# A fused attention, gating and MLP kernel: plain float32 scores and zero products in the first batch, earlier loads, and a clamp moved to GpSimd

## The chip, the cores and the metric

The kernel runs on one core of one Trainium2 chip. The metric is the device time of one launch in microseconds (us). The kernel before takes 788.62 us, the median of three runs (787.88 to 788.93). Engines are named as the profile names them: PE is TensorE (matrix products), PEld its weight loads, DVE is VectorE, ACT is ScalarE, POOL is GpSimd, SP is the engine whose queue issues all DMAs here.

## The reference

Three stages, in float32, for 4 batches of 576 positions:

```python
# 1: causal attention with a decay, 8 heads of 64 (32 heads in all)
scores = q @ k.T / 8 ; bias = -(cum[i] - cum[j]), cum = cumsum(max(s, 0))
scores = where(causal, -1e9, scores + min(bias, 0))
attn = exp(scores - max) / (sum + 1e-9) ; x = attn @ v      # heads side by side: 576 x 512
# 2: gated product
gate = sigmoid(causal 5-tap convolution of x, per channel) ; x = (gate * (x @ w_val)) @ w_out
# 3: mixing along the sequence at rank 32, then a two-layer MLP
u = x + (x.T @ U @ V).T ; out = u + max(u @ w_ch1, 0) @ w_ch2        # 512 -> 2048 -> 512
```

The inputs of stages 2 and 3 come as 64-bit floats, so weights are read as pairs of 32-bit words.

## The kernel before

**Precision.** PE can take a float32 operand whole, or in a reduced form (`F32R`). Most products here run in the reduced form on a high and a low part of each operand: the rounded value and the rest. For scores this means two products: row block Q1 with K1 (high parts, and four rows that carry the decay) and Q2 with K2 (the cross terms). A head listed in `WHOLE` (line 85) skips this: q and k go straight into Q1 and K1, and one plain float32 product makes a score block. In the trace a plain product stands as two MATMUL records.

**Splitting q and k.** For a head not in `WHOLE`, `load_head` (line 274) loads q and k into one tile `qk` by two DMAs, and `prep_head` (line 296) makes `hi` on ACT (`qk_hi`), the rest on POOL (`qk_lo`, tile Q2), and issues five DMAs on SP's queue that put the parts where the products want them. `load_head(n + 1)` stands at the start of step n of the main loop (line 736), so `qk` is loaded one head ahead.

**A head.** Five query chunks. `score` makes a chunk's scores, DVE masks them and takes the row minimum (`nm`; tile P), ACT takes the exponential (with the sum), `trans` transposes P in up to four blocks of 128 by 128 through a PSUM tile `pt`, six groups to a head, ACT or DVE copies them out to PTA or PTB, and `attn_v` multiplies with V for two heads at once (`av`). `norm_rows` (line 546) brings the sums of a pair of heads into rows: DVE makes a reciprocal, POOL spreads it (`wrs`), PE transposes it, and ACT or DVE copies it back. `norm` (line 564) then makes X, its high and low part (`xh` on POOL, `xl` on POOL), and the gate by five taps.

**Side work.** Weights are widened from 64-bit words by `widen` (line 350), nine steps for each half: scale on ACT (`wd_a`), clamp on DVE (`wd_lim`), four bit operations on DVE (`wd`), rounding, rest and low part on POOL. In the attention stage this goes step by step beside the heads. From 330 us on, `widen_w` (line 807) does the rest of the MLP weights, two halves for each of 14 blocks; each half starts with a DMA of 512 KB into the tile `raw`.

**Dense work.** From the ninth head on, stages 2 and 3 (up to `u`) of the batch before run beside the heads; the MLP itself (`ch1`, `ch2`: tiles `d`, `hh`, `hl`, `acc`) begins around 330 us and fills the rest.

**What sets the order.** `PLAN` and `FIRST` give the engine and a priority to each kind of work; `defer` holds work back by the planner's own clock with the delays in `DT`. A scheduler then orders each engine's instructions. Each engine, and SP's queue of DMA issues, runs its list in order; an instruction that waits holds up all behind it.

Of the kernel before, what the change touches and what calls it, by code (L numbers as in the profile page):

```python
# [11 lines left out]
F32 = mybir.dt.float32  # L12
# [21 lines left out]
    "ul": ("gpsimd", -6000),  # L34
    "u4": ("vector", 0),
    "wd_a": ("scalar", 6000),
    "wd_lim": ("vector", -100),
    "wd": ("vector", -2000),
    "wd_hi": ("gpsimd", -2000),
    "wd_lo": ("gpsimd", 2000),  # L40
# [41 lines left out]
RING = 7  # L82
PACED = False
SIDE = [7, 7, 3, 7]
WHOLE = [0, 1, 2, 3, 16, 30]
PB = [1, 1, 1, 2, 2]
XB = 1
FIRST = {"pt41": ["scalar", 500], "nl": ["vector", 500], "xh": ["gpsimd", 2000], "c2": ["tensor", 100], "max": ["vector", 2000], "rs": ["vector", 500], "t": ["tensor", 100], "rb": ["vector", 500], "av": ["tensor", 6000], "wd_rest": ["gpsimd", 2000]}
ORDER0 = "T0 S0 T1 T4 S1 T3 T2 S2 S3 S4"
ORDER = "T0 T1 S0 T2 T3 S1 S2 S3 T4 S4 A0 A1"  # L90
NPD = 6
DT = {"exp": 0.51, "xh": 0.96, "xl": 0.25, "tap": 1.5, "taps": 0.9, "tanh": 1.83, "gv": 4.3, "nl": 3.6, "rows": 7.68, "prep": 1.51}
WARM = 13


# [1 line left out]
def fused_kernel(ctx, tc, qT, kT, vP, s, wval, wout, convw, U, V, w1, w2, rows01, out):  # L97
# [173 lines left out]

    hd = {}

    def load_head(n, direct=False):
        b, h = divmod(n, H)
        t = hd[n] = {"K": 64 + KP if n else 66, "nm": at.tile([P, 6], F32, tag="nm", name="nm")}
        kind = F32 if n in WHOLE else F32R
        for nm in ("Q1", "K1"):
            t[nm] = at.tile([64 + KP, S], kind, tag=nm, name=nm)
        if n in WHOLE:  # L280
            q, k = t["Q1"][0:64, :], t["K1"][0:64, :]
        else:
            t["qk"] = at.tile([P, S], F32, tag="qk", name="qk")
            q, k = t["qk"][0:64, :], t["qk"][64:, :]
        nc.sync.dma_start(q, qT[b, h])
        nc.sync.dma_start(k, kT[b, h])
        if n:
            for i, nm in enumerate(("Q1", "K1")):
                nc.sync.dma_start(t[nm][64:, :].bitcast(F32), EF[i][n:n + 1] if direct else ef[n, i])
# [87 lines left out]
    def pairs(t):  # L377
        return t.bitcast(U32).rearrange("p (n two) -> p n two", two=2)
# [78 lines left out]
        side_work.append(lambda j=j: widen_half(j))  # L457


    def score(n, c):  # L460
        t = hd[n]
        W, q0, r = CW[c], Q0[c], QN[c]
        regions = [(0, W)] if c < 4 else [(0, HS), (HS, S)]
        shift = S - P - (W - r if c else 0)
        nm = t["nm"]
        pr = Pt[c][n % PB[c]]
        force("sc", 1)
        worst = 3.0e38
        for i, (k0, k1) in enumerate(regions):
            ps = psD.tile([P, 512], F32, tag="d", name="sc")  # L470
            o = ps[:, 0:k1 - k0]
            if n in WHOLE:
                K = t["K"]
                Via("s").matmul(o, t["Q1"][0:K, q0:q0 + P], t["K1"][0:K, k0:k1], start=True, stop=True)
            else:
                Via("s").matmul(o, t["Q1"][:, q0:q0 + P], t["K1"][:, k0:k1], start=True, stop=False)
                Via("s").matmul(o, t["Q2"][:, q0:q0 + P], t["K2"][:, k0:k1], start=False, stop=True)
            last = k1 == W
            least = nm[0:r, c:c + 1] if last else nm[0:r, 5:6]

            Via("max").tensor_tensor_reduce(
                pr[0:r, k0:k1], o[0:r, :], causal[0:r, k0 + shift:k1 + shift], -0.125, worst,
                op0=ALU.add, op1=ALU.min, accum_out=least,
            )
            worst = least

        def exp():
            Via("exp").activation(
                pr[0:r, 0:W], pr[0:r, 0:W], AF.Exp, bias=nm[0:r, c:c + 1], scale=-1.0,
                accum_out=sums[n // 2 % 2][0:r, c, n % 2:n % 2 + 1],  # L490
            )
            ready.add(("P", n, c))
        defer(DT["exp"] + W / 960.0, exp, "sc")

    def trans(n, c):
        w, q0 = QN[c], Q0[c]
        nblk = c + 1
        until(("P", n, c))
        if c == 0:
            hd[n]["PTA"] = at.tile([P, 4 * DA], F32, tag="PTA", name="PTA")  # L500
            hd[n]["PTB"] = at.tile([P, 5, S - SA], F32, tag="PTB", name="PTB")
        groups = [(0, nblk)] if nblk <= 4 else [(0, 3), (3, 5)]
        for b0, b1 in groups:
            force("pt", 1)
            ps = psD.tile([P, 512], F32, tag="d", name="pt")
            for j in range(b0, b1):
                Via("t").transpose(ps[:, (j - b0) * P:(j - b0 + 1) * P], Pt[c][n % PB[c]][:, j * P:(j + 1) * P], ident)
            if q0 < SA:
                dst = hd[n]["PTA"][:, q0:q0 + b1 * DA].rearrange("p (j w) -> p j w", w=DA)[:, b0:b1, 0:w]
            else:  # L510
                dst = hd[n]["PTB"][:, b0:b1, q0 - SA:q0 - SA + w]
            src = ps[:, 0:(b1 - b0) * P].rearrange("p (j w) -> p j w", w=P)[:, :, 0:w]
            rnd(f"pt{c}{b0 // 3}", dst, src)
# [32 lines left out]
    def norm_rows(pr):  # L546
        force("sc")
        sm = sums[pr % 2]
        rs = at1.tile([P, 5, 2], F32, tag="rs", name="rs", bufs=2)
        Via("rs").tensor_scalar_add(rs, sm, 1e-9)  # L550
        Via("rs").reciprocal(rs, rs)
        wide_rs = at1.tile([P, 5, P], F32, tag="wrs", name="wrs")
        rnd("wrs", wide_rs.rearrange("p c (e d) -> p c e d", e=2), rs.unsqueeze(3).to_broadcast([P, 5, 2, 64]))
        ready.add(("rows", pr))
        RB = RBs[pr] = wide_rs.rearrange("p c q -> p (c q)")[:, 0:S]
        for lo, hi, cs in ((0, SA, (0, 1, 2)), (SA, S, (3, 4))):
            ps = psD.tile([P, 512], F32, tag="d", name="pt")
            for c in cs:
                w, o = QN[c], Q0[c] - lo

                Via("t_rb").transpose(ps[:, o:o + P], wide_rs[:, c, :], ident)
            rnd("rb", RB[:, lo:hi], ps[:, 0:hi - lo])
# [173 lines left out]
    for n in range(NH + 1):  # L736
# [2 lines left out]
            pace[:] = [hd[n - 1]["nm"][:, 4:5]]  # L739
        if 2 <= n + 1 < NH:  # L740
            load_head(n + 1, n == 1)
        if n == 1:
            nc.sync.dma_start(craw.bitcast(U32), words(convw))
        if 1 <= n <= 3:
# [59 lines left out]
    reuse = dict(bufs=1, reuse_waits="tile")  # L804
    wa = ctx.enter_context(tc.tile_pool(name="wa", side="right", **reuse))

    def widen_w(m):
        pool = w0 if m % RING < 2 else wb if m % RING < 4 else ml
        d = w12[m] = {x: pool.tile([P, TW], F32R, tag=f"{x}{m % RING}", name=x) for x in ("w1h", "w1l", "w2h", "w2l")}

        def part(nm, src):
            raw = raw1 if nm == "w1" else wb.tile([P, 2 * TW], F32, tag="raw", name="raw")
            nc.sync.dma_start(raw.bitcast(U32), src)
            scr = [wa.tile([P, TW], F32, tag=f"scr{k}", name=f"scr{k}", bufs=2 - k) for k in range(2)]
            return widen(pairs(raw), scr, hi=d[nm + "h"], lo=d[nm + "l"])
        return [
            lambda: part("w1", words(w1)[m]), lambda: part("w2", words(w2)[m * P:(m + 1) * P, :]),
            lambda: ready.add(m),
        ]

# [95 lines left out]
    ctx_b.close()  # L916
    wb = ctx.enter_context(tc.tile_pool(name="wb", side="right", **reuse))
    beside(outputs(B - 1), R2)
    for _ in first_blocks:
        pass  # L920
    ctx_a.close()
# [51 lines left out]
```

## Time and profile before

| | |
|---|---|
| median of three runs | 788.62 us |
| profiled execution | 789.94 us, of it the span 788.1 us |
| PE busy | 744.9 us (95%) |
| DVE busy | 481.9 us (61%) |
| ACT busy | 300.0 us (38%) |
| POOL busy | 271.6 us (34%) |
| mean granted PE clock | 0.97 |

PE is busy nearly all the time from 100 us on. In the first 100 us it is not, and there its granted clock is below 0.9 in every slice of the page. Times within the trace count from the start of the span. A timeline row gives the start, the length, the engine, line, operation and tiles, how many instructions it merges, and in brackets how long the engine stood idle before it and whose work ended that.

### The profile page before, as it was taken

Reading aid. Unit: us, or ns where it says so; the run is one execution under the profiler, and the core shown is the slowest. Engines: PE = TensorE matmul, PEld = TensorE weight load, DVE = VectorE, ACT = ScalarE, POOL = GpSimd, SP = SyncE. Lnnn points to the kernel's source line nnn. Section 1 sums busy time; section 2 is a strip of 40 time slices with the busy share of each in tenths; the row PEclk is TensorE's granted clock in tenths of the full one; section 3 lists DMA queues with packets and bytes.
Section 4 is the critical chain, followed back from the end, with each engine's and each line's share of the span. In section 5 each row is a group of like instructions: output and inputs, shape, how many; then the busy total and the mean of one; then the engine's idle time right before and its main releaser. Section 6 shows DMA issues by size and latency. Waiting matters only on the chain.

```text
span 788.1 us, 12200 instructions
## 1 busy us (share of the span) xinstructions
PE 744.9 (95%) x4341; PEld 625.1 (79%) x4341; DVE 481.9 (61%) x1100; ACT 300.0 (38%) x789; POOL 271.6 (34%) x277
## 2 busy tenths in 40 slices
PE   7877889989999999999999989999999999999998
PEld 4666778768897999799778768888878888888887
DVE  5688887588856765676748995823593233422334
ACT  4776566666578677733202211201121011101100
POOL 2366555344332333538176651301350012200000
PEclk8887799989999999999999999999999999999999
DMA  5756544544445543012102320200030000000023
GB/s 150 217 155 186 135 123 106 140 125 114 115 108 142 146 103 79 18 40 95 54 1 81 107 81 27 80 1 27 9 109 17 0 27 1 2 1 0 1 107 133
DMA packets 28612, 62.34 MB, mean 79 GB/s; under 512 B 4974, under 2 KB 5614, under 8 KB 28552
## 3 DMA queue, kind: packets, MB, share of 16 engines
q1 hardware_dynamic: 28552, 61.57, 28.1%
q8 instruction: 34, 0.56, 0.3%
q14 instruction: 26, 0.21, 0.1%
HBM read 37.04 MB, written 5.31 MB: 54 GB/s over the span
## 4 chain that ended last, share of the span: by engine, by line
PE 69%; DVE 12%; DMA 6%; ACT 5%; POOL 3%; issue 2%; SPq 1%; ACTq 0%; DVEq 0%; POOLq 0%
PE d L132 31%; PE acc L132 21%; DVE scr L132 7%; PE pt L132 7%; PE av L132 5%; PE sc L132 5%; DMA qk<-in_kT 2%; DVE uT L132 2%; DMA K<-Q 2%; ACT P L132 2%; DMA raw<-in_w 1%; POOL u L132 1%; DVE hl L132 1%; POOL Q L132 1%; ACT PTB L132 1%
## 5 line engine op out<-in xcount | busy, mean ns | idle before, releaser
L132 PE MATMUL d<-u,w1h 128*128 128x512 f32 (+1 forms) x640 | 185.2, 373 | 4.9 <-DVE hl L132 4.9
L132 DVE SCALAR_TENSOR_TENSOR hl<-d,hh 128x512 fp32r<-128x512 f32 (+1 forms) x80 | 50.5, 634 | 161.9 <-ACT hh L835 161.8
L835 ACT ACTIVATE hh<-d 128x512 fp32r<-128x512 f32 (+1 forms) x80 | 44.1, 554 | 265.5 <-PE acc L132 140.1
L132 PEld LDWEIGHTS d<-u,w1h 128*128 128x128 f32 x640 | 116.3, 189 | 28.4 <-DVE hl L132 6.6
L132 PE MATMUL d<-u,w1l 128*128 128x512 f32 (+1 forms) x320 | 119.0, 372 | 0.0
L132 PE MATMUL acc<-hl,w2h 128*128 128x512 f32 (+1 forms) x320 | 105.1, 373 | 0.1
L132 PE MATMUL sc<-K,Q 68*128 68x288 f32 (+11 forms) x384 | 93.9, 358 | 11.5 <-ACT PTB L132 5.1
L132 PE MATMUL acc<-hh,w2h 128*128 128x512 f32 (+1 forms) x320 | 104.0, 372 | 0.5 <-DVE uT L132 0.5
L132 PE MATMUL acc<-hh,w2l 128*128 128x512 f32 (+1 forms) x320 | 102.2, 371 | 0.0
L132 ACT ACTIVATE P<-P,nm 64x64 f32<-64x64 f32 (+4 forms) x160 | 89.1, 560 | 29.5 <-DVE nm L132 29.1
L132 PE MATMUL pt<-ident,P 128*128 128x128 f32 x480 | 79.5, 296 | 8.1 <-ACT P L132 5.4
L132 DVE TENSOR_TENSOR uT<-acc,uT 128x512 f32<-128x512 f32 (+1 forms) x120 | 70.3, 629 | 23.4 <-PE acc L132 23.2
L132 DVE CUSTOM_DVE_ANT_0 P<-sc,causal 64x64 f32<-64x64 f32 (+4 forms) x160 | 65.2, 421 | 30.0 <-PE sc L132 24.5
L132 PEld LDWEIGHTS sc<-K,Q 68*128 68x128 f32 (+2 forms) x384 | 67.1, 210 | 19.5 <-ACT PTB L132 6.3
L132 DVE TENSOR_SCALAR scr<-scr 128x512 uint32<-128x512 uint32 (+1 forms) x84 | 61.9, 742 | 17.5 <-POOL w1l L132 9.2
L132 PEld LDWEIGHTS pt<-ident,P 128*128 128x128 f32 x480 | 58.7, 151 | 17.4 <-ACT P L132 9.3
L132 PEld LDWEIGHTS d<-u,w1l 128*128 128x128 f32 x320 | 60.7, 190 | 11.0
L132 PEld LDWEIGHTS acc<-hh,w2h 128*128 128x128 f32 x320 | 58.9, 188 | 12.1 <-issue 0.9
L132 PEld LDWEIGHTS acc<-hl,w2h 128*128 128x128 f32 x320 | 59.0, 189 | 11.6 <-DVE hl L132 0.5
L132 PEld LDWEIGHTS acc<-hh,w2l 128*128 128x128 f32 x320 | 58.7, 188 | 11.3
L132 POOL TENSOR_TENSOR Q<-qk,hi 128x576 fp32r<-128x576 f32 x26 | 38.1, 1464 | 63.1 <-PE sc L132 24.1
L588 DVE SCALAR_TENSOR_TENSOR av<-X,cw,av 128x576 f32<-128x576 f32 x64 | 52.1, 814 | 3.5 <-ACT av L132 3.3
(119 smaller groups left out, 1261.4 us busy)
## 6 DMA issues: line engine op xcount, KB each, us to landing
raw<-in_w SPq DMA_DIRECT2D x28, 512.0 KB
K<-hi SPq DMA_DIRECT2D x52, 144.0 KB
Q<-hi SPq DMA_DIRECT2D x52, 144.0 KB
V<-in_vP SPq DMA_DIRECT2D x16, 320.0 KB
out<-uT SPq DMA_DIRECT2D x16, 256.0 KB
qk<-in_qT SPq DMA_DIRECT2D x26, 144.0 KB
qk<-in_kT SPq DMA_DIRECT2D x26, 144.0 KB
K<-Q SPq DMA_DIRECT2D x26, 144.0 KB
```

Of the source, the lines that this page charges most:

```text
L132: return f(*args, **kw)
L588: Via("tap").scalar_tensor_tensor(g, X[:, k:k + S], cw[:, p, k:k + 1], g, op0=ALU.mult, op1=ALU.add,)
L835: Via("hh").activation(h_, o, AF.Relu)
```

## The change

- Heads 4 to 7 join `WHOLE`, so all eight heads of the first batch are scored in plain float32, and are no longer split.
- `fill` (new) puts two products of zeros (bf16, 128 by 128 with 256 columns) ahead of each group of transposes, and of each of the two groups in `norm_rows`, as long as the main loop is at most at step 8. They go into the PSUM tile that the transposes then write. 112 such products stand in PE's list.
- `load_raw` (new) loads the `qk` tile of a head that is split two heads ahead instead of one.
- `load_w` (new) issues the DMA of a weight half as soon as the sixth step of the half two before it has read its tile, instead of at the half's own start.
- The clamp `wd_lim` goes from DVE to POOL.
- `norm_rows` is held back by 10.0 instead of 7.68 of the planner's units.

```diff
-    "wd_lim": ("vector", -100),
+    "wd_lim": ("gpsimd", 0),
-WHOLE = [0, 1, 2, 3, 16, 30]
+WHOLE = [0, 1, 2, 3, 4, 5, 6, 7, 16, 30]
-DT = {..., "rows": 7.68, "prep": 1.51}
+DT = {..., "rows": 10.0, "prep": 1.51}
...
+    raw = {}
+    def load_raw(n):
+        if n < NH and n not in WHOLE:
+            b, h = divmod(n, H)
+            raw[n] = at.tile([P, S], F32, tag="qk", name="qk")
+            nc.sync.dma_start(raw[n][0:64, :], qT[b, h])
+            nc.sync.dma_start(raw[n][64:, :], kT[b, h])
     def load_head(n, direct=False):
...
         if n in WHOLE:
-            q, k = t["Q1"][0:64, :], t["K1"][0:64, :]
+            nc.sync.dma_start(t["Q1"][0:64, :], qT[b, h])
+            nc.sync.dma_start(t["K1"][0:64, :], kT[b, h])
         else:
-            t["qk"] = at.tile([P, S], F32, tag="qk", name="qk")
-            q, k = t["qk"][0:64, :], t["qk"][64:, :]
-        nc.sync.dma_start(q, qT[b, h])
-        nc.sync.dma_start(k, kT[b, h])
+            t["qk"] = raw.pop(n)
...
+    def fill(ps, n):
+        if phase[0] <= H:
+            for _ in range(n):
+                Via("t").matmul(ps[:, 0:256], warm[:, 0:P], warm[:, 0:256], start=True, stop=True)
...
             ps = psD.tile([P, 512], F32, tag="d", name="pt")
+            fill(ps, 2)
             for j in range(b0, b1):
...
             load_head(n + 1, n == 1)
+        load_raw(n + 2)
...
+    raws = {}
+    def load_w(k):
+        m = k // 2
+        if m < NF:
+            raws[k] = wb.tile([P, 2 * TW], F32, tag="raw", name="raw") if k % 2 else raw1
+            nc.sync.dma_start(raws[k].bitcast(U32), words(w2)[m * P:(m + 1) * P, :] if k % 2 else words(w1)[m])
...
-        def part(nm, src):
-            raw = raw1 if nm == "w1" else wb.tile([P, 2 * TW], F32, tag="raw", name="raw")
-            nc.sync.dma_start(raw.bitcast(U32), src)
+        def part(nm, k):
             scr = [wa.tile([P, TW], F32, tag=f"scr{k}", name=f"scr{k}", bufs=2 - k) for k in range(2)]
-            return widen(pairs(raw), scr, hi=d[nm + "h"], lo=d[nm + "l"])
+            steps = widen(pairs(raws.pop(k)), scr, hi=d[nm + "h"], lo=d[nm + "l"])
+            return steps[:6] + [lambda: load_w(k + 2)] + steps[6:]
```

How instructions move, at three places. First PE, where the scores of head 4 begin beside the transposes of head 3 (`P_89` and so on are the exponentials). Before, each score block is a pair of products (K1 with Q1, then K2 with Q2):

```order
L132 MATMUL sc<-K_371,Q_370 128x64
L132 MATMUL sc<-K_381,Q_380 128x64
L132 MATMUL pt<-ident,P_89 128x128 x3
L132 MATMUL pt<-ident,P_91 128x128 x4
L132 MATMUL sc<-K_371,Q_370 128x192
L132 MATMUL sc<-K_381,Q_380 128x192
L132 MATMUL sc<-K_371,Q_370 128x320
L132 MATMUL sc<-K_381,Q_380 128x320
```

Now, the same place; a row on `causal` is a zero product or its weight load:

```order
L132 MATMUL sc<-K_399,Q_398 128x64
L132 LDWEIGHTS causal
L132 MATMUL pt<-causal 128x256
L132 LDWEIGHTS causal
L132 MATMUL pt<-causal 128x256
L132 MATMUL pt<-ident,P_89 128x128 x3
L132 LDWEIGHTS causal
L132 MATMUL pt<-causal 128x256
L132 LDWEIGHTS causal
L132 MATMUL pt<-causal 128x256
L132 MATMUL sc<-K_399,Q_398 128x192
L132 MATMUL pt<-ident,P_91 128x128 x4
```

One product stands for a pair, and two zero products stand ahead of the group of transposes.

Second ACT, from the exponentials of head 2 (first row) to the first ones of head 4. Before:

```order
L132 ACTIVATE P_92,sums_97<-P_92,nm 128x576
L139 ACTIVATE PTA<-pt 128x64
L132 ACTIVATE PTA<-pt 128x2x128
L132 ACTIVATE av<-X_94,cw 128x576
L132 ACTIVATE hi<-qk 128x576
L132 ACTIVATE PTB<-pt 128x3x128
L132 ACTIVATE PTB<-pt 128x2x128
L132 ACTIVATE P_87,sums_97<-P_87,nm 64x64
L132 ACTIVATE PTB<-pt 128x4x128
```

Now:

```order
L132 ACTIVATE P_92,sums_97<-P_92,nm 128x576
L139 ACTIVATE PTA<-pt 128x64
L132 ACTIVATE av<-X_94,cw 128x576
L132 ACTIVATE PTA<-pt 128x2x128
L132 ACTIVATE P_87,sums_97<-P_87,nm 64x64
L132 ACTIVATE PTB<-pt 128x3x128
L132 ACTIVATE PTB<-pt 128x2x128
L132 ACTIVATE uT<-uT 128x512
```

The instruction `hi`, which waits for a load of q and k, no longer stands between the exponentials and the copies to PTB. The heads 8 and 9, the first that are split now, have their `hi` in places 4 and 19 of ACT's list, heads 4 and 5 had them there before.

Third DVE in the MLP, around a step `hl`, on which the next products of PE wait; the names in brackets are what a row waits for. Before, DVE does the clamp (the first of two TENSOR_SCALAR in place on a `scr`), which waits for ACT:

```order
L132 TENSOR_SCALAR scr_5941<-scr_5940 128x512 [waits DVE_49,Pool_49]
L132 SCALAR_TENSOR_TENSOR scr_5941<-raw,scr_5941 128x512 [waits DVE_49]
L132 TENSOR_SCALAR scr_5992<-scr_5992 128x512 [waits Activation_49]
L132 TENSOR_SCALAR scr_5992<-scr_5992 128x512 [waits DVE_49]
L132 SCALAR_TENSOR_TENSOR scr_5992<-raw_4465,scr_5992 128x512 [waits DMAHW5_49,DVE_49]
L132 SCALAR_TENSOR_TENSOR hl<-d,hh 128x512 [waits Activation_49]
```

Now, and below it POOL around one clamp:

```order
L132 TENSOR_SCALAR scr_6000<-scr_6000 128x512 [waits Pool_49]
L132 SCALAR_TENSOR_TENSOR scr_6000<-raw,scr_6000 128x512 [waits DMAHW0_49,DVE_49]
L132 TENSOR_SCALAR scr_6001<-scr_6000 128x512 [waits DVE_49,Pool_49]
L132 SCALAR_TENSOR_TENSOR scr_6001<-raw,scr_6001 128x512 [waits DVE_49]
L132 SCALAR_TENSOR_TENSOR hl<-d,hh 128x512 [waits Activation_49]
```

```order
L365 TENSOR_SCALAR scr_6000<-scr_6000 128x512 [waits Activation_49]
L132 TENSOR_TENSOR w1l<-scr_5947,scr_5948 128x512 [waits DVE_49,Pool_49]
L132 TENSOR_SCALAR w2h<-scr_6000 128x512 [waits DVE_49,PE_49]
L365 TENSOR_SCALAR scr_6058<-scr_6058 128x512 [waits Activation_49]
L132 TENSOR_TENSOR scr_6000<-scr_6000,w2h 128x512 [waits DVE_49,Pool_49]
```

The clamp stands in POOL's list between the low and high part of two other halves, and DVE's first operation on a half waits for POOL.

## Rows read from the trace of the kernel before

**Rows 1.** The page, the clock granted to PE in 40 slices of 19.7 us, in tenths
```profile
PEclk8887799989999999999999999999999999999999
```

**Rows 2.** Busy time by stage: stretch, its length, engines, granted clock, DMA share, GB/s
```profile
12.00:93.50 81.50, 65.23 (x391) 52.18 (x391) 58.40 (x174) 55.31 (x163) 41.14 (x36) 0.78 0.66 177
93.50:330.00 236.50, 226.59 (x1704) 197.37 (x1704) 170.31 (x513) 162.50 (x474) 94.99 (x101) 0.99 0.45 113
330.00:500.00 170.00, 161.69 (x862) 136.48 (x861) 128.03 (x208) 40.79 (x79) 93.35 (x88) 0.99 0.18 60
500.00:788.10 288.10, 283.68 (x1364) 235.38 (x1362) 115.28 (x186) 36.46 (x65) 36.30 (x32) 1.00 0.10 33
```

**Rows 3.** Busy time in stretches at a full and at a reduced clock, same columns
```profile
18.00:34.90 16.90, 14.32 (x95) 10.15 (x93) 12.51 (x46) 10.59 (x32) 7.05 (x7) 1.00 0.81 227
...
72.50:89.50 17.00, 14.25 (x63) 11.38 (x65) 13.43 (x38) 11.94 (x37) 10.89 (x9) 0.50 0.65 166
...
171.50:178.30 6.80, 6.80 (x22) 5.14 (x21) 4.64 (x14) 2.29 (x8) 1.06 (x2) 0.50 0.16 54
465.00:468.40 3.40, 3.40 (x16) 3.11 (x15) 3.40 (x7) 0.00 (x0) 1.20 (x2) 0.50 0.02 5
```

**Rows 4.** Timeline of PE, its waits, 35 to 84 us
```profile
35.29 2.29 PE L132 MATMUL sc<-K,Q 68*128 68x288 f32 x4 [2.02 <-ACT PTB L132]
...
55.09 1.87 PE L132 MATMUL pt<-ident,P 128*128 128x128 f32 x7 [1.18 <-ACT P L132]
...
62.36 1.33 PE L132 MATMUL pt<-ident,wrs 128*128 128x128 f32 x5 [2.46 <-POOL wrs L132]
...
72.57 2.08 PE L132 MATMUL sc<-K,Q 68*128 68x448 f32 x6 [2.64 <-ACT PTB L132]
...
84.01 1.33 PE L132 MATMUL pt<-ident,wrs 128*128 128x128 f32 x5 [2.54 <-POOL wrs L132]
```

**Rows 5.** Timeline of ACT, the split of q and k
```profile
34.18 0.68 ACT L132 ACTIVATE hi<-qk 128x576 fp32r<-128x576 f32 x1 [2.88 <-DMA K<-ef]
...
71.45 0.68 ACT L132 ACTIVATE hi<-qk 128x576 fp32r<-128x576 f32 x1 [2.41 <-DMA qk<-in_kT]
```

**Rows 6.** Timeline of POOL ahead of the wait at 59.9 us
```profile
60.04 1.41 POOL L132 TENSOR_TENSOR Q<-qk,hi 128x576 fp32r<-128x576 f32 x1 [0.46 <-PE sc L132]
61.41 0.90 POOL L132 TENSOR_SCALAR wrs<-rs 128x640 f32<-128x640 f32 x1
```

**Rows 7.** Timeline of PE, scores of three larger chunks, plain then split
```profile
17.52 2.60 PE L132 MATMUL sc<-K,Q 68*128 68x320 f32 x8
...
51.10 1.50 PE L132 MATMUL sc<-K,Q 68*128 68x320 f32 x8
```

**Rows 8.** Timeline of PE, five transposes, then two of the first dense products
```profile
46.80 0.77 PE L132 MATMUL pt<-ident,wrs 128*128 128x128 f32 x5
...
93.64 0.29 PE L132 MATMUL d<-xl,wvh 128*128 128x288 f32 x1
93.77 0.29 PE L132 MATMUL d<-xh,wvl 128*128 128x288 f32 x1
```

**Rows 9.** Timeline of all engines around the longest wait after 330 us
```profile
460.59 0.67 ACT L132 ACTIVATE scr<-raw 128x512 f32<-128x512 f32 x1 [6.71 <-DMA raw<-in_w]
...
461.30 1.95 DVE L132 TENSOR_SCALAR scr<-scr 128x512 f32<-128x512 f32 x2 [0.90 <-ACT scr L132]
...
463.88 0.68 DVE L132 SCALAR_TENSOR_TENSOR hl<-d,hh 128x512 fp32r<-128x512 f32 x1
...
464.62 0.50 PE L132 MATMUL d<-u,w1h 128*128 128x256 f32 x2 [3.00 <-DVE hl L132]
```

**Rows 10.** DVE by shape, the clamp: late weights, then first batch
```profile
L132 DVE TENSOR_SCALAR scr<-scr 128x512 f32<-128x512 f32 x28 | 23.0, 820 | 5.4 <-ACT scr L132 5.4
...
L132 DVE TENSOR_SCALAR uT<-uT 128x512 f32<-128x512 f32 x8 | 3.7, 459 | 3.6 <-ACT uT L132 3.6
```

**Rows 11.** POOL by shape, rounding of the late weights
```profile
L132 POOL TENSOR_SCALAR w1h<-scr 128x512 fp32r<-128x512 f32 x14 | 9.3, 662 | 120.4 <-DVE hl L132 52.7 <-PE d L132 45.4 <-DVE scr L132 22.3
```

More of the change, by code (lines that the diff above doesn't have):

```diff
@@ L91 @@
 NPD = 6
-DT = {"exp": 0.51, "xh": 0.96, "xl": 0.25, "tap": 1.5, "taps": 0.9, "tanh": 1.83, "gv": 4.3, "nl": 3.6, "rows": 7.68, "prep": 1.51}
+DT = {"exp": 0.51, "xh": 0.96, "xl": 0.25, "tap": 1.5, "taps": 0.9, "tanh": 1.83, "gv": 4.3, "nl": 3.6, "rows": 10.0, "prep": 1.51}
 WARM = 13
@@ L557, in norm_rows @@
             ps = psD.tile([P, 512], F32, tag="d", name="pt")
+            fill(ps, 2)
             for c in cs:
@@ L809, in widen_w @@
         d = w12[m] = {x: pool.tile([P, TW], F32R, tag=f"{x}{m % RING}", name=x) for x in ("w1h", "w1l", "w2h", "w2l")}
-        def part(nm, src):
-            raw = raw1 if nm == "w1" else wb.tile([P, 2 * TW], F32, tag="raw", name="raw")
-            nc.sync.dma_start(raw.bitcast(U32), src)
+        def part(nm, k):
             scr = [wa.tile([P, TW], F32, tag=f"scr{k}", name=f"scr{k}", bufs=2 - k) for k in range(2)]
-            return widen(pairs(raw), scr, hi=d[nm + "h"], lo=d[nm + "l"])
+            steps = widen(pairs(raws.pop(k)), scr, hi=d[nm + "h"], lo=d[nm + "l"])
+            return steps[:6] + [lambda: load_w(k + 2)] + steps[6:]
         return [
-            lambda: part("w1", words(w1)[m]), lambda: part("w2", words(w2)[m * P:(m + 1) * P, :]),
+            lambda: part("w1", 2 * m), lambda: part("w2", 2 * m + 1),
             lambda: ready.add(m),
@@ L918, in fused_kernel @@
     beside(outputs(B - 1), R2)
+    for k in (4, 5):
+        load_w(k)
     for _ in first_blocks:
```

## The prediction

> **What bounds the kernel now.** I read the clock line of the page first, then the busy time by stage, then the waits of PE in the timeline, and last what ACT, POOL and DVE did at these places. The clock is below 0.9 in the first five slices and nearly full after them [rows 1]. By stage, PE is the bound from 93.5 us on: 226.6 of 236.5 us, 161.7 of 170, 283.7 of 288.1 [rows 2]. There nothing can win more than PE's idle time and the little that a reduced clock costs. The stretch from 12 us to the first dense products at 93.6 us [rows 8], the first batch alone, is another matter: PE is busy for 65.2 of 81.5 us, DVE for 58.4, ACT for 55.3, and the clock's mean is 0.78. No engine is full, so the waits between them count, and PE works part of the time at 1.2 GHz, the lower of its two levels. A mean of 0.78 over 81.5 us is 0.22 x 2 x 81.5 = 36 us at half clock. The longest piece, 72.5 to 89.5 us, has the clock at 0.50 throughout with PE busy for 14.25 of 17 us [rows 3].
>
> **The first batch: what goes.** Five waits of PE stand in rows 4: 2.02, 1.18, 2.46, 2.64 and 2.54 us, 10.8 of the 16.3 us that PE idles in this stretch. Two of them end on PTB, a copy by ACT, and in front of both ACT stood still for `hi`, which waited 2.88 and 2.41 us for its load or for the step before it [rows 5]. Two end on `wrs` by POOL, and in front of the first POOL did the rest of q and k for 1.41 us before it came to `wrs` at 61.41 us [rows 6]; the second looks alike. The fifth ends on an exponential that ACT came to late. With heads 4 to 7 no longer split, neither instruction is there. The heads that are still split, from 8 on, have theirs long before they are needed, since their loads go out two heads ahead. So I take the 10.8 us as gone, and 16.3 - 10.8 = 5.5 us of idle time as left. What is late next is DVE: 58.4 us of work here less some clamps, which is under 80% of the length I come to, so it doesn't bind.
>
> **The clock.** PE's work at half clock is 36 us times 14.25/17, some 30 us. Five transposes take 1.33 us inside the half-clock piece and 0.77 us in a stretch at full clock [rows 4, 8], so a full clock gives back up to half, 15 us, and leaves 65.2 - 15 = 50 us of the present work. Will it be full? The long piece at half clock starts at the wait of 2.64 us that I expect to go [rows 3, 4]. From 18 to 34.9 us, where the scores of the plain heads 1 to 3 run, the clock is 1.00 with PE busy for 14.3 of 16.9 us [rows 3]. Four more plain heads and the zero products bring the later heads nearer to that. I take nine tenths of the time as full.
>
> The Trainium skill, in "TensorE: Matmul & The Clock Gate", Part 4 on transposes, says that a transpose doesn't count as PE being busy in the way a product does, for the clock. The trace agrees as far as it goes: PE was busy for 84% of the 17 us, much of it with transposes, and the clock stayed at half [rows 3]. By that rule the zero products, which are ordinary products, are what keeps the clock up; without it they would be dead weight, which is the third rival below.
>
> **What it adds to PE.** Eight records of scores (320, 448 and twice 288 columns, two records each) take 2.60 us plain and 1.50 us split [rows 7]. That is 1344 of a head's 1600 columns, so a plain head costs 1.10 x 1600/1344 = 1.3 us more, four heads 5.2 us. A zero product passes over 256 columns; two dense products of 288 columns start 0.13 us apart [rows 8], so one is some 0.12 us and 112 are 13 us at full clock, at half twice that. A part of them falls into waits for exponentials, where it costs nothing.
>
> **Sum for the first batch.** 50 + 5.2 + 13 = 68 us of work on PE at full clock; 1.5 us for the tenth of the time at half; 5.5 us idle: 75 us instead of 81.5, so -6. The low end has the idle time filled by zero products and the clock full: 68, -13. The high end has the clock as now: 65.2 + 18.2 x 1.3 + 5.5 = 94, +13. I stay in the half of the low end, for the full clock of the plain heads.
>
> **From 93.5 to 330 us.** PE idles for 9.9 us [rows 2], and 6.8 us at half clock from 171.5 on [rows 3] cost 3.4. Loads of q and k two heads ahead take `hi` off its DMA, and the clamps of the side work leave DVE (8 x 0.46 us [rows 10]; the smaller ones likewise). The waits here are many small ones with different causes, and `norm_rows` comes later, so X may too. I take -2, with -6 and +4 as ends.
>
> **From 330 us on.** The longest wait is one of 3.00 us for `hl`. The rows behind it read backwards: `hl` at 463.88 stands behind two operations on a weight half, whose first waited for ACT, which had stood 6.71 us for the DMA into `raw` [rows 9]. The clock then falls to half for 3.4 us [rows 3], another 1.7. With the DMA issued a half earlier, these 4.7 us should go. The other idle time of this stage (8.3 us in all up to 500 us [rows 2]) has other causes, and the 4.4 us after 500 us are mostly the end, where nothing changes.
>
> Against it stands the clamp. On DVE it takes 0.82 us for a half among the late weights and 0.46 among the early ones [rows 10]; DVE loses 28 x 0.82 = 23 us. On POOL the nearest operation, a rounding of the same shape, takes 0.66 us [rows 11], so POOL gains 18.5 us. The rest of the half now waits for POOL in DVE's list, with `hl` behind it. A POOL operation ahead of it can last 1.4 us (the rest of q and k is of that kind [rows 6]). From 0 (the clamp ready in time) to 28 x 1.4 = 39 us (each half held up by a whole operation, and PE with it), I take the price near its low end, 1.2 us, because PE works two steps behind and stood only 8.3 us here with a DVE that was 75% busy (128 of 170 us [rows 2]) and now has less to do. So -3.5 for this part, with -8 and +6 as ends.
>
> The Trainium skill, in "Advanced Engine Details and Errata", VectorE Performance Modes, says that GpSimd instructions and VectorE's two-port ones get in each other's way at a shared SBUF port. This speaks against more work on POOL: the bit operations that stay on DVE could be held longer. The trace agrees that something of the kind happens, with 0.82 us for a clamp where POOL works beside and 0.46 for one of the same shape earlier [rows 10].
>
> **Sum.** The profiled execution took 789.94 us: -6, -2 and -3.5 make 778.4. It lies 1.3 us above the median of the three runs (788.62), so 777 for the median.
>
> **Rivals.**
> *More of it.* The idle time is filled by the zero products, the waits after 93.5 us that hang on loads all go: -13 - 5 - 6 = -24, 764.6 for the median. For it: the 112 products stand right in front of transposes that wait for an exponential. Against: waits with other causes stay.
> *Given back.* A head is paced by the chain from scores over maximum, exponential and transposes to the copy, and the products added lengthen it as much as the stalls shorten it: 0 for the first batch, -2 for the rest: 786.6. For it: DVE and ACT are at 72 and 68% of the first stretch [rows 2].
> *Slower by the clock.* Place: 12 to 93.5 us. The clock stays as it is, 36 us at half, and 18 us of new products cost 1.3 times as much: +13, of which zero products in waits take back 3; -2 for the rest: 797. It decides when the clock's mean there stays under about 0.85. For it: 17 us at half clock under an 84% busy PE. Against: the plain heads from 18 to 34.9 us.
> *Slower by the clamp.* Place: 330 to 500 us and the widening after it. POOL's rounding stood 45.4 us for products of PE that still read the old weights [rows 11], and the next clamp now stands behind such a row; DVE and `hl` wait with it. If nine of the 28 halves cost PE 1.4 us each, +12.6 against -8: 793. It decides from 8/28 = 0.3 us a half.
>
> **How the numbers follow.** Forecast 0.55, with 771 to 784 as its own range; more of it 0.15; given back 0.15; slower by the clock 0.08; slower by the clamp 0.07. The range of 767 to 791 leaves out the greater part of the first rival's low side and of the slower cases. A measurement can tell about 0.2%, 1.6 us, from no change: faster has the forecast, the first rival and two thirds of the second, 0.80; same 0.06; slower 0.14.
>
> **What would show it.** Right: the first dense products, at 93.6 us before, come some 6 us earlier; the mean clock from 12 us to there is above 0.9; PE's waits on `wrs` and on PTB are gone from the first batch; no `raw` wait of 6 us by ACT, and no wait of 3 us on `hl` in the MLP. Wrong: a clock as before, or PE idle in the first batch beside the zero products; in the MLP, DVE waiting on `scr` from POOL ahead of `hl`; or a loss in the dense stage, where X waits for `rb`.

## The result, and the profile after

| | before | after |
|---|---|---|
| median (lowest to highest) | 788.25 us (785.09 to 788.93), 4 runs | 765.85 us (764.29 to 768.24), 4 runs |
| profiled execution, its span | 789.94, 788.1 | 764.93, 762.8 |
| mean granted clock | 0.970 | 0.993 |
| ratio, 95% interval | | 0.9727 (0.9701 to 0.9753) |

The change took 22.4 us off the median where 11.6 were forecast, and the time lies 1 us below the range. What came is the size of the first rival, "more of it" (764.6), though not for its reasons, so its size is in good part luck. Measured once more among the experiments, on another chip, the changed kernel took 767.98 us, ratio 0.9743 (0.9712 to 0.9773).

Three marks in the trace divide the time in the same way for every kernel: the start of DVE's X of the fourth pair of heads (the end of the first batch), that of the sixteenth pair (the last), and the end of PE's last product. First the busy time between these marks before (columns as in [rows 2]), then after.

```profile
12.00:90.80 78.80, 62.53 (x369) 49.53 (x370) 55.70 (x166) 53.20 (x158) 39.33 (x34) 0.77 0.67 179
90.80:340.00 249.20, 238.06 (x1795) 206.77 (x1795) 179.34 (x539) 169.60 (x489) 103.88 (x110) 0.99 0.43 108
340.00:785.00 445.00, 436.58 (x2155) 365.11 (x2153) 236.54 (x374) 72.26 (x132) 122.58 (x111) 1.00 0.13 43
```

```profile
12.00:79.20 67.20, 65.52 (x479) 50.35 (x480) 51.26 (x158) 50.71 (x153) 35.71 (x37) 0.97 0.56 158
79.20:324.20 245.00, 236.22 (x1794) 206.38 (x1795) 177.56 (x525) 171.06 (x491) 109.63 (x125) 0.99 0.44 112
324.20:759.50 435.30, 433.31 (x2155) 364.11 (x2153) 224.77 (x346) 72.98 (x132) 139.85 (x139) 1.00 0.13 44
```

The first batch is 11.6 us shorter: PE works 3 us more, at a clock of 0.97 for 0.77, and its idle time falls from 16.3 to 1.7 us. The dense attention stage is 4.2 us shorter, the MLP stage 9.7. In the MLP stage DVE has 28 instructions less and POOL 28 more: the clamps.

The page's clock line after, to be held against [rows 1], stands at 9 (0.9 or more) in each slice.

```profile
PEclk9999999999999999999999999999999999999999
```

In PE's timeline after, the transposes of `wrs` stand without a wait (2.46 and 2.54 us in [rows 4]), and the first dense product, at 93.6 us in [rows 8], comes at 81.94.

```profile
62.66 0.71 PE L132 MATMUL pt<-ident,wrs 128*128 128x128 f32 x5
...
75.67 0.77 PE L132 MATMUL pt<-ident,wrs 128*128 128x128 f32 x5
...
81.94 0.30 PE L132 MATMUL d<-xh,wvh 128*128 128x288 f32 x1
```

In the MLP stage before the change, the waits of PE for `hl` from 330 us on (what waits, for whom: us in total, times, longest), then the moment from which `hl` could have started in [rows 9], the end of `hh`:

```profile
PE d L132 <- DVE hl L132: 6.2, 5, 3.0
```

```profile
461.17 0.58 ACT L835 ACTIVATE hh<-d 128x512 fp32r<-128x512 f32 x1
```

After the change no wait of PE for `hl` is left. The place that answers to [rows 9], a timeline of ACT, POOL and DVE:

```profile
443.53 0.68 ACT L132 ACTIVATE scr<-raw 128x512 f32<-128x512 f32 x1 [5.98 <-DMA raw<-in_w]
...
444.11 0.58 ACT L861 ACTIVATE hh<-d 128x512 fp32r<-128x512 f32 x1
...
444.74 0.94 POOL L365 TENSOR_SCALAR scr<-scr 128x512 f32<-128x512 f32 x1
...
445.12 0.68 DVE L132 SCALAR_TENSOR_TENSOR hl<-d,hh 128x512 fp32r<-128x512 f32 x1
445.73 1.50 DVE L132 TENSOR_SCALAR scr<-scr 128x512 uint32<-128x512 uint32 x1
```

ACT still stands 5.98 us for `raw`. But `hl` starts 0.4 us after `hh` has ended, and the bit operations on the new half come behind it. In [rows 9] the clamp and two bit operations stand between (the row x2 merges the clamp and the first of them), and `hl` starts 2.1 us after `hh` has ended: DVE waits 0.90 us for ACT's `scr`, and the three operations then take 2.6 us. DVE's waits say the same, before from 340 to 500 us and after from 324 to 484:

```profile
DVE hl L132 <- ACT hh L835: 14.3, 6, 3.2
...
DVE scr L132 <- ACT scr L132: 4.4, 4, 2.2
```

```profile
DVE hl L132 <- ACT hh L861: 22.0, 11, 7.5
```

DVE's waits for ACT's `scr` are gone. It now more often reaches `hl` ahead of `hh`.

### The profile page after: what moved, and what is told of

It reads as the page before. It is cut to its first block, busy times and chain, and to the rows that moved or that the text cites. A ratio compares the mean times of both kernels' runs of the same rounds, so it can differ in the third digit from the quotient of the medians.

```text
span 762.8 us, 12349 instructions
## 1 busy us (share of the span) xinstructions
PE 743.7 (98%) x4453; PEld 624.8 (82%) x4453; DVE 464.4 (61%) x1052; ACT 299.2 (39%) x785; POOL 291.2 (38%) x321
## 4 chain that ended last, share of the span: by engine, by line
PE 85%; DMA 4%; DVE 4%; ACT 3%; issue 2%; SPq 1%; POOL 0%; ACTq 0%; DVEq 0%
PE d L132 39%; PE acc L132 26%; PE pt L132 8%; PE av L132 6%; PE sc L132 6%; DMA qk<-in_kT 2%; DMA K<-Q 1%; DVE av L604 1%; ACT P L132 1%; DVE P L132 1%; DMA Q<-hi 1%; DVE uT L132 1%; DMA uT<-in_w 0%; ACT PTB L132 0%; ACT hi L132 0%
## 5 line engine op out<-in xcount | busy, mean ns | idle before, releaser
L132 PE MATMUL sc<-K,Q 68*128 68x288 f32 (+11 forms) x384 | 89.1, 344 | 4.6 <-ACT PTB L132 1.8
L132 DVE CUSTOM_DVE_ANT_0 P<-sc,causal 64x64 f32<-64x64 f32 (+4 forms) x160 | 65.2, 421 | 30.8 <-PE sc L132 28.2
L132 PEld LDWEIGHTS sc<-K,Q 68*128 68x128 f32 (+2 forms) x384 | 62.2, 193 | 13.2 <-ACT PTB L132 2.6
L132 PEld LDWEIGHTS acc<-hh,w2h 128*128 128x128 f32 x320 | 58.7, 188 | 12.1 <-issue 0.9
L132 PEld LDWEIGHTS pt<-ident,P 128*128 128x128 f32 x480 | 56.3, 145 | 12.3 <-ACT PTA L139 3.6
L132 DVE SCALAR_TENSOR_TENSOR scr<-raw,scr 128x512 uint32<-128x512 uint32 (+1 forms) x56 | 52.4, 936 | 1.4
L132 DVE TENSOR_SCALAR scr<-scr 128x512 uint32<-128x512 uint32 x56 | 43.3, 773 | 11.9 <-POOL w1l L132 6.3
```

The lines of the kernel that those rows point to most:

```text
L132: return f(*args, **kw)
```

## The experiments

There are eighteen runs: sixteen kernels, one of them twice (e6, r2), and the changed one again (r1). Each has its ratio to the kernel before, measured beside it, the start of the fourth X, the length from the fourth X to the sixteenth (dense), and the MLP stage from there to PE's last product. The three lengths are from one profiled execution each. The runs f2, e7, g1, g4 and h4 stand in the text only. The texts of e3, f1, f2 and e8 count the MLP stage to the end of the span, 3.3 us later: 438.6 there is 435.3 here.

| run | parts of the change in it | median us | ratio (95%) | 4th X | dense | MLP |
|---|---|---|---|---|---|---|
| before | none | | 1 | 90.8 | 249.2 | 445.0 |
| f1 | clamp | 785.04 | 0.9966 (0.9942 to 0.9989) | 95.8 | 248.2 | 435.3 |
| h2 | heads 4 to 7 | 782.58 | 0.9913 (0.9887 to 0.9939) | 86.5 | 245.6 | 444.3 |
| h3 | zero products | 788.82 | 0.9999 (0.9976 to 1.0022) | 95.5 | 243.6 | 444.8 |
| h1 | clamp, heads | 772.90 | 0.9772 (0.9741 to 0.9804) | 88.3 | 244.2 | 435.3 |
| g2 | clamp, heads, zero | 766.68 | 0.9714 (0.9681 to 0.9747) | 79.7 | 243.7 | 435.3 |
| e4 | all but clamp | 788.15 | 0.9993 (0.9970 to 1.0017) | 88.1 | 248.3 | 444.8 |
| e2 | all but heads | 778.59 | 0.9860 (0.9829 to 0.9891) | 92.3 | 245.6 | 435.4 |
| e1 | all but zero | 776.21 | 0.9811 (0.9765 to 0.9857) | 80.3 | 252.5 | 435.3 |
| e8 | clamp, loads, rows | 787.66 | 0.9987 (0.9963 to 1.0012) | 96.7 | 252.7 | 435.3 |
| e3 | all, weights late | 769.91 | 0.9758 (0.9722 to 0.9794) | 80.8 | 247.5 | 435.3 |
| e6, r2 | all but rows | 764.35, 765.51 | 0.9689, 0.9708 | 78.8, 79.2 | 243.5, 246.9 | 435.3 |
| r1 | all | 767.98 | 0.9743 (0.9712 to 0.9773) | 79.0 | 247.3 | 435.3 |

**One part taken back at a time.** e1 has `fill` with 0 for 2. e2, e3 and e4 are these, each in the changed kernel:

```
-WHOLE = [0, 1, 2, 3, 4, 5, 6, 7, 16, 30]
+WHOLE = [0, 1, 2, 3, 16, 30]
```

```
         def part(nm, k):
+            load_w(k)
...
-            return steps[:6] + [lambda: load_w(k + 2)] + steps[6:]
+            return steps
...
-    for k in (4, 5):
-        load_w(k)
```

```
-    "wd_lim": ("gpsimd", 0),
+    "wd_lim": ("vector", -100),
```

> The changed kernel without its 112 zero products; all else as changed (765.9 us). What I hold: plain scores of heads 4 to 7 and the zero products keep the clock up together, so without the products some 15 to 20 us of the first batch run at half clock again, which costs 5 to 8 us, and the products' own 13 us were mostly spent in waits or paid by the clock: X of the fourth pair (79.2 us after the change, 90.8 before) comes at 82 to 87, total 769 to 774. Rival, the plain scores hold the clock alone and the products are dead weight: X of the fourth pair at 70 to 76 with the clock as it is, total 757 to 763. Rival, the products only stand in waits: within 1.5 us of 765.9, PE idle longer by about the 13 us.

> The changed kernel with heads 4 to 7 split again, zero products and loads as changed. What I hold: PE's waits on wrs and on the copies to PTB come back in part (two heads ahead the loads are early, so those on hi's load not), PE saves 5.2 us of plain scores: X of the fourth pair at 80 to 86 us, total 767 to 773, mean clock of the first stretch 0.85 to 0.95. Rival, the zero products hold the clock alone and the plain scores only add work: X of the fourth pair at 74 to 78, total 761 to 765. Rival, the plain scores hold the clock alone: mean clock of the first stretch under 0.85, X of the fourth pair at 88 or later, total 775 or more.

> The changed kernel with each MLP weight half loaded when its own widening starts, as before the change; clamp on GpSimd. What I hold: ACT waits 5 to 7 us for the DMA into raw again and the wait on hl with the dip of the clock behind it returns: the MLP stage, which came 9.5 us earlier with the change, loses 5 to 9 of them; total 771 to 775, the first batch unchanged. Rival, the clamp on GpSimd is what freed hl: within 1.5 us of 765.9 although ACT waits.

> The changed kernel with the clamp of the widening back on DVE; weights loaded early. What I hold: the clamp is nearly free on either engine as PE works two steps behind: 764 to 767.5. Rival, DVE freed of 28 clamps is what lets hl come in time in the MLP stage: 770 to 775, with waits of PE on hl back. Rival, the shared port: the bit operations on DVE, 773 ns with the clamp on GpSimd against 703 before, fall back and the total is 1 to 3 us lower.

e4 decided against me: the clamp, which I held nearly free on either engine, is worth 22 us in this company. The MLP stage is back at 444.8. The weights are loaded early here, and yet the chain of [rows 9] is back, row by row, in e4's timeline:

```profile
457.23 0.67 ACT L132 ACTIVATE scr<-raw 128x512 f32<-128x512 f32 x1 [6.91 <-DMA raw<-in_w]
...
457.93 1.87 DVE L132 TENSOR_SCALAR scr<-scr 128x512 f32<-128x512 f32 x2 [0.97 <-ACT scr L132]
...
460.45 0.68 DVE L132 SCALAR_TENSOR_TENSOR hl<-d,hh 128x512 fp32r<-128x512 f32 x1
...
461.19 0.60 PE L132 MATMUL d<-u,w1h 128*128 128x256 f32 x2 [3.01 <-DVE hl L132]
```

e3 is the counterpart: late weights, clamp on GpSimd. ACT waits as long, and nobody waits behind it:

```profile
447.73 0.68 ACT L132 ACTIVATE scr<-raw 128x512 f32<-128x512 f32 x1 [5.77 <-DMA raw<-in_w]
...
449.26 0.68 DVE L132 SCALAR_TENSOR_TENSOR hl<-d,hh 128x512 fp32r<-128x512 f32 x1
```

Its MLP stage is 435.3 us, so the early weight loads bring nothing there. The trace shows why: they don't leave earlier. Before the change too, the DMA of a half goes out when DVE has last read the tile `raw` that it overwrites. First before, then after, DVE's last read of a `raw`, the issue of the next DMA, and ACT's read of what it brings:

```profile
459.70 0.69 DVE L132 SCALAR_TENSOR_TENSOR scr<-raw,scr 128x512 f32<-128x512 uint32 x1
...
460.46 0.33 SPq L813 DMA_DIRECT2D raw<-in_w  x1
...
463.85 0.66 ACT L132 ACTIVATE scr<-raw 128x512 f32<-128x512 f32 x1 [2.10 <-DMA raw<-in_w]
```

```profile
444.22 0.98 DVE L132 SCALAR_TENSOR_TENSOR scr<-raw,scr 128x512 f32<-128x512 uint32 x1
...
445.26 0.33 SPq L831 DMA_DIRECT2D raw<-in_w  x1
...
448.86 0.68 ACT L132 ACTIVATE scr<-raw 128x512 f32<-128x512 f32 x1 [2.40 <-DMA raw<-in_w]
```

Of the 27 issues that follow such a read, 26 before the change, 27 after it and 26 in e3 come within 0.1 us of its end, and the median from issue to ACT's read is 3.3 to 3.5 us in all three. The 4 us of e3's median lie before the MLP stage, and the interval of its ratio overlaps that of the whole change. In e2 the heads are worth 13 us, more than I held (773 at most) and as much as their rival said, though the products kept the clock of its first stretch at 0.90. In e1 the products are worth some 10, with executions from 767 to 779 us and clocks from 0.989 to 0.975. The profiled one (773.22 us) loses 1.1 us of this up to the fourth X and 7.5 in the dense stage, against the changed kernel's 79.2 and 245.0.

**The clamp alone, and the engine against the order.** f1 is the kernel before with e4's line the other way round. f2 is e4 with 0 for -100. e8 is the changed kernel with `fill` at 0 and heads 4 to 7 split, e7 has `fill` at 1.

> The kernel before with one line changed: the clamp of the widening on GpSimd, nothing else (no zero products, heads 4 to 7 split, loads as before). New theory, from the run with the clamp back on DVE: the clamp's engine alone sets the MLP stage, because on DVE it is the instruction that waits for ACT's scr and so stands in front of hl. Then from X of the sixteenth pair to the end it takes 438.6 us as after the change (448.1 before), the waits on hl are gone, and the total is 776 to 780; X of the fourth pair stays at 88 to 92. Rival, my prediction's price (clamp costs, early weight loads gain): 788 to 791, MLP stage 448 or more. Rival, the clamp pays only together with the early weight loads: MLP stage 443 to 448, total 783 to 788.

> The changed kernel with the clamp on DVE at scheduling priority 0, not -100 as before the change: tells the engine from the order, as the change altered both numbers of the entry. If the engine counts: as with -100, 786 to 790, waits of PE on hl there, MLP stage 447 to 449. If the order counts (the lower priority had put the clamp where it blocks hl): 765 to 771, MLP stage near 439.

> The changed kernel without zero products and with heads 4 to 7 split as before: the clamp on GpSimd, the early loads and the rows figure are left. Taking out the products alone cost 10 us and splitting the heads alone 13; if these two only pay together (each needed to keep the clock up), the loss here is about that of one of them: 776 to 780, X of the fourth pair at 89 to 92. If each has its own gain that adds up: 786 to 790. The MLP stage is at 438.6 us in both.

> The changed kernel with one zero product per group in place of two (56 for 112). If the products work by filling waits and holding the clock, half of them hold it in part: 766 to 774, with executions spread between the two as without any (767 to 779). If the second of each pair only adds to PE: X of the fourth pair 3 to 6 us earlier, 760 to 764.

f2 took 789.82 us, ratio 1.0006 (0.9981 to 1.0031), MLP stage 443.9: it is the engine, not the priority. f1 has the MLP stage at 435.3 by one changed line, but a first batch 5 us longer, so the total was 785, outside what I expected. Its timeline shows what the clamp costs there (ACT, POOL and DVE, from two stretches of the first batch):

```profile
43.28 1.42 POOL L132 TENSOR_TENSOR Q<-qk,hi 128x576 fp32r<-128x576 f32 x1 [2.12 <-PE sc L132]
...
48.77 1.26 POOL L132 TENSOR_TENSOR wvl<-uT 128x512 fp32r<-128x512 f32 x1
...
50.07 0.66 ACT L132 ACTIVATE uT<-uT 128x512 f32<-128x512 f32 x1 [3.75 <-POOL wvl L132]
...
50.81 0.61 POOL L357 TENSOR_SCALAR uT<-uT 128x512 f32<-128x512 f32 x1 [0.78 <-ACT uT L132]
...
51.46 0.43 DVE L132 TENSOR_SCALAR uT<-uT 128x512 uint32<-128x512 uint32 x1 [3.89 <-POOL uT L357]
```

POOL's rest of q waits for PE's scores, the widening waits behind it on POOL, ACT for the scratch tile, and DVE, with the maxima behind it, for the clamp. PE's waits in f1's first batch are for the most part on ACT, 9.6 us on PTA and 6.5 on `uT`. With plain heads POOL has no such rests. e8 landed where I had put "each has its own gain that adds up" (787.66), but not for that reason: its first batch and dense stage lose what the MLP gains. e7 took 773.87 us, ratio 0.9816 (0.9790 to 0.9843), fourth X 81.2, dense 252.0: no better than none.

**Is it DVE's load, or the clamp's place in its list?**

```
     lambda: (
         Via("wd").tensor_scalar(tu, au, 0xFF800000, None, op0=ALU.bitwise_and),
+        Via("wd").tensor_scalar(t, t, 3.0e38, -3.0e38, op0=ALU.min, op1=ALU.max),
     ),                                            (g1)
```

g2 is the kernel before with f1's line, h2's heads and `fill(ps, 2)`. g4 has `fill` at 1 up to head 5, and e6 has rows at 7.68.

> The changed kernel (clamp on GpSimd) with a second, useless clamp on DVE in every weight half, put on the other scratch tile after the fifth step, where DVE has no wait: DVE has as many widening operations as before the change, but none of them is the first to read what ACT wrote. If what counts is the clamp's place in DVE's list (it waits there for ACT's scr, which waits for the DMA, with hl and the maxima behind it): the MLP stage stays at 435.3 us to PE's last product (445.0 before), X of the fourth pair at 79 to 82, total 765 to 770. If DVE's load counts: MLP stage 442 to 446, X of the fourth pair at 86 to 89, total 780 to 790.

> The kernel before with three of the parts alone: the clamp on GpSimd, heads 4 to 7 plain, the zero products. No load of q, k or weights moved, rows as before. If the early loads bring nothing: 764 to 769, as the whole change. If q and k two heads ahead are worth something in the dense attention stage (245.0 us from the fourth X to the sixteenth with the change): 249 to 253 there, total 770 to 775; the MLP stage is at 435.3 in either case.

> The changed kernel with one zero product per group up to head 5 and two from head 6 on. With one everywhere X of the third pair came at 61.3 (64.7 with two), but the clock fell at 72.2 us and the fourth came at 81.2, and the dense stage took 252.0 for 245.0. If the products matter for the clock only at the end of the batch, where the scores run out: X of the fourth pair at 75 to 77, total 761 to 764, faster than the whole change. If their number or the placing of other work by it matters throughout: 768 to 775.

> The changed kernel with the figure rows back at 7.68 (norm_rows taken up earlier after its head). If it was moved only to fit the rest: within 2 us of 765.9. If rows at 10.0 is what shortened the dense attention stage from 249.2 to 245.0: that stage at 248 to 251, total 769 to 772. First batch and MLP as with the change.

g1 took 771.89 us, ratio 0.9779 (0.9743 to 0.9814). Its two outer stages (as above):

```profile
12.00:82.60 70.60, 68.75 (x494) 53.63 (x494) 54.94 (x169) 51.08 (x154) 38.27 (x38) 0.95 0.58 161
327.80:764.20 436.40, 433.77 (x2154) 364.20 (x2152) 239.52 (x374) 73.18 (x132) 136.29 (x139) 1.00 0.13 44
```

DVE has 374 instructions in the MLP stage, as before the change, and is busy 3 us longer than then, and still the stage takes 436.4 us for 445.0. So some 8.6 of the 9.7 us are the clamp's place and 1.1 DVE's load, though the total lies 2 us above what I put for the place. No run leaves the clamp on DVE and puts `hl` ahead of it, so it isn't shown that another engine is needed for this; another priority alone (f2) doesn't do it. In the first batch the load costs 3.4 of the 8.9 us by which e4 is behind. g2 has the whole gain without any early load. g4 took 769.01 us, ratio 0.9759 (0.9725 to 0.9792), fourth X 77.2, dense 251.1: the 2 us of its first batch were given back.

**Which part turns the clamp from a loss into a gain.** h1 to h3 are the parts named in the table, put into the kernel before. h4 is g4 with rows at 7.68.

> The kernel before with two parts: the clamp on GpSimd and heads 4 to 7 plain; no zero products, loads and rows as before. If the plain heads are what turns the clamp's 5 us of loss in the first batch into a gain (GpSimd no longer has the rests of q and k of four heads in front of the clamp and DVE's wait on it): X of the fourth pair at 79 to 83, total 767 to 774. If the zero products do it: 88 or later, total 775 or more.

> The kernel before with heads 4 to 7 plain and nothing else. What I forecast in the first batch came from this part first of all (the waits on wrs and PTB gone, a full clock). If it does that without the clamp moved: X of the fourth pair at 82 to 87 (90.8 before), total 780 to 785. If DVE, whose list still has the clamp in front, then holds PE back: 87 to 90, total 784 to 789.

> The kernel before with the 112 zero products and nothing else. If they hold the clock by themselves: mean clock of the first batch from 0.77 to 0.9 or more, X of the fourth pair at 86 to 90, total 783 to 788. If they only add to PE while waits go on: 91 to 98, total 789 to 797.

> The changed kernel with one zero product per group up to head 5, two from head 6 on, and rows at 7.68. With rows at 7.68 and all products the dense attention stage took 243.5 us, with fewer early products and rows at 10.0 it took 251.1. If rows is what the stage then hangs on: 243 to 246 there, X of the fourth pair near 77, total 760 to 764, the fastest so far. If the number of early products sets how the rest is placed: 249 to 253, total 766 to 771.

h2 came as I had put it for heads that do it without the clamp. h1 came between: its total is the heads', its fourth X the products'. Beside the clamp, the heads gave 12.1 us of median (785.04 to 772.90) and the products on top 6.2; by the ratios, which allow for the different chips, 15 and 5. The intervals of h1 and g2 touch, so the products' part is clear only from e1 against the whole change (0.9765 to 0.9857 for 0.9701 to 0.9753). Without the clamp the heads gave 6 (their ratio 0.9913), and the kernel with heads, products and loads (e4) nothing. The products alone (h3) raised the clock of the first batch from 0.77 to 0.92, and its end came 4.7 us later. The first batch of h1, then that of g2, shows what they do beside the rest:

```profile
12.00:88.30 76.30, 67.65 (x374) 49.16 (x375) 49.31 (x153) 51.47 (x151) 33.46 (x34) 0.78 0.48 135
```

```profile
12.00:79.70 67.70, 64.09 (x479) 49.12 (x480) 51.26 (x158) 50.56 (x153) 35.77 (x37) 1.00 0.58 157
```

With 105 instructions more PE is busy 3.6 us less, since the clock is 1.00 for 0.78. This pair is one execution each. In e1, where the clock is 0.90 without products, PE is busy for 57.84 us up to the fourth X, 7.7 less than in the changed kernel. The Trainium skill ("TensorE: Matmul & The Clock Gate", Part 4) says that a transpose doesn't count as PE being busy in the same way. The trace of h1 agrees: PE is busy for 89% of the stretch, 147 of its 374 instructions are transposes, and the mean clock is 0.78. But e1 has 147 of 375 and 0.90, so the rule alone doesn't give the clock. The fourth X came at 88.3 in h1 and at 80.3 in e1, whose median is the higher of the two; whether that is chance or their different lists, one execution of each doesn't show.

h4 took 766.18 us, ratio 0.9719 (0.9673 to 0.9766), dense 250.3: it is not rows that makes this stage longer with fewer products.

**The changed kernel and the one without rows, on one chip.**

> The changed kernel itself, beside the next one on the same chip: 764 to 768, X of the fourth pair near 79, dense stage near 245, MLP 435.3.

> The changed kernel with rows at 7.68, the fastest so far (764.35), beside the changed kernel on the same chip. If rows matters: 1 to 3 us below it, with the dense attention stage at 243 to 244 for 245. If the figure is without effect: within 1 us of it, intervals of the ratios overlapping.

r2's ratio is 0.9708 (0.9673 to 0.9742). Its median is 2.5 us below r1's, as e6's 0.9689 (0.9661 to 0.9716) is below the change's, with overlapping intervals: nothing faster than the changed kernel is shown, though rows at 10.0 has nothing to say for it. The changed kernel's dense stage is 245.0 in one profiled execution and 247.3 in the other, so 2 us there are no difference. Still open is why it took 250.3 to 252.7 us in all five kernels with early loads and less than all the products (e1, e7, e8, g4, h4), and 243.5 to 249.9 in all others. The order of the instructions in the stage differs between them. No run separates that from the loads. The loads of q and k, too, hardly leave earlier: from the issue of the second DMA into `qk` to `hi` the median is 3.4 us in the changed kernel and 3.4 in g2, which loads one head ahead.

## Why the prediction was wrong

- **The clamp** is the step that failed. I took its price "near its low end, 1.2 us", a loss, with "PE works two steps behind" as the cover. It is the largest gain: -9.7 us in the MLP stage by itself (f1), and 22 us of median beside the other parts (e4 against the change). I had the row in front of me: in [rows 9] DVE's wait for ACT ends in the clamp, with two bit operations and `hl` behind it, and [rows 10] put 5.4 us of waits for ACT to the clamps. I read the first wait of that chain, for the DMA, as the cause. After the change ACT's longest wait is still 5.98 us. What mattered is who stands next in line: on GpSimd the clamp is still released by ACT's `scr`, but `hl` isn't queued behind it. I also counted only the longest of PE's five waits for `hl`, 3.0 of 6.2 us, and gave the others "other causes". All five went, and with the clock PE's busy time in this stage fell from 436.6 to 433.3 us: 6.4 us of idle time and 3.3 of work for my 3.0 and 1.7.
- **"With the DMA issued a half earlier, these 4.7 us should go"**: they went, for the other reason, and the DMA is not issued a half earlier: it waits for the tile, before as after. With the loads early and the clamp on DVE all of it is still there (e4); with the loads late and the clamp moved it is gone (e3, f1). ACT's waits for `raw` in this stage fell from 65.2 to 41.9 us in all, but go by the clamp too: 64.5 in e4, 43.5 in e3.
- **The sum of the first batch** (75 us to the first dense products; 69.9 came). PE's work came as forecast, 66.9 us at full clock in g2 for my 68, and so did the clock, 0.98 for 0.9 or more. The term off is "5.5 us idle": 1.7 were left. That term too needs the clamp, which I had ruled out with "so it doesn't bind", from DVE's load alone. With it on DVE (e4) PE idles for 7.4 us up to the fourth X, 5.0 of them waiting for DVE's `nm` (1.4 after the change), and DVE's waits on ACT's `uT`, 5.0 us in all before, are 7.8. An example from DVE's timeline in e4, with X behind the clamp:

```profile
66.95 0.43 DVE L132 TENSOR_SCALAR uT<-uT 128x512 f32<-128x512 f32 x1 [2.22 <-ACT uT L132]
67.29 0.75 DVE L132 TENSOR_TENSOR X<-av,wrs 128x576 f32<-128x576 f32 x1
```

- **The dense stage** was forecast at -2 (-6 to +4); -4.2 and -1.9 came in two executions. Right within its spread, but the loads of q and k aren't the reason: g2, without them, has 243.7. Nor do they give heads 8 and 9 their `hi` early: it starts at 10.1 and 21.1 us in both kernels.
- **What drives the first batch** was half right: the plain heads and the products together hold the clock, each alone does so in part (0.82 in h2, 0.92 in h3, 0.98 in e4). But a full clock without the clamp moved gave 2.7 us of the fourth X (88.1 in e4), not 6: PE then waits for DVE.
- **The rivals.** "Slower by the clamp" named the right place and the wrong sign; GpSimd's clamps did wait for ACT, 13.8 us among the late weights after the change, without harm there. "Slower by the clock" fell with the clock at 0.97. "Given back" is what e4 does in total. "More of it" came out in size: the idle time filled, as it said, but not "the waits that hang on loads". It had -13, -5 and -6 us; -11.6, -4.2 and -9.7 came.
- **The shared port.** The reasoning fits the traces, and cost no time. Before the change DVE's late clamps take 0.42 us where POOL is idle (7 of the 28) and 0.95 where POOL works beside them. With the clamp on POOL, DVE's bit operations with one input on `scr` went from 703 to 773 ns in the MLP stage, and those that read `scr` and `raw` from 831 to 936, 56 x 0.105 = 5.9 us of DVE's time. The Trainium skill, in "Advanced Engine Details and Errata", VectorE Performance Modes, says that GpSimd instructions and VectorE's two-port ones interfere at the port they share. The slower clamp and bit operations beside POOL's work agree with that; that they are two-port ones, no trace here shows. PE was the bound there with 433.3 of 435.3 us.

## What to carry to other kernels

On an engine that works through its list in order, the instruction that first reads another engine's late result holds up everything behind it. Such an instruction can be worth moving to an engine where less urgent work stands behind it, even where it takes longer there (0.61 us on GpSimd for 0.46 on DVE among the early weights); count what stands behind the wait, not the instruction's own time. Count also what stands in front of it on the new engine: behind the rests of q and k the same move cost 5 us of the first batch (f1). Parts of a change that each remove one of several limits of a stage can't be priced one by one: here the clamp, the heads and the products gave 4, 6 and 0 us alone and about 22 together. And where a chain begins with a long wait, look whether that wait is still there in a kernel that doesn't suffer from it, before calling it the cause; and before moving a load ahead in the program, look in the trace what its issue waits for.

## What was not expected of the hardware

- Asking for the weight loads earlier did not end ACT's wait for them: its longest was 5.98 us after the change, 6.91 in e4 and 5.77 with the loads late (e3). In each of these kernels nearly every DMA into `raw` left within 0.1 us of DVE's last read of the tile.
- 112 products that do nothing went with a shorter busy time of PE in one pair of executions, 64.1 for 67.7 us in the first batch (g2 against h1): the clock was at 2.4 GHz throughout, where its mean without them was 0.78. In the other pair, the change against e1 with a clock of 0.90, PE was busy longer, 65.5 for 57.8 us.
